# Retention and a routed mixture of experts on one core: slots by rank of the token count, experts chosen by register, short last blocks with slots as columns

## The chip, the cores and the metric

One NeuronCore of a Trainium2 chip runs the whole program. The metric is device time in microseconds of one execution, lower is better. The span is the stretch of a profiled execution in which the program's instructions run; the execution's own time is a little longer.

## The reference

Two stages. The first is attention without softmax, with a decay per head; the second sends each token to one expert. B, H, S, D = 4, 8, 576, 64; 2304 tokens of 512 features; 8 experts with inner size 1024; capacity 576.

```
scores = q k^T / sqrt(64);  ret = scores * gamma_h ** (i - j) for i >= j, else 0
x = (ret v), heads side by side                       # 2304 x 512
logits = x w_gate;  e(i) = argmax(logits_i);  p = softmax(logits)
slot of token i = number of earlier tokens with the same expert
h = relu(x w1[e]);  y = h w2[e];  out_i = p_i[e(i)] * y   # 0 where the slot is >= capacity
```

## The kernel before

**Attention stage (0 to 124 us).** A loop over 20 tiles of tokens (NTI; 5 of a batch, the last of them half full). Each tile's rows of x are written to DRAM (`xr`) as pairs of float16, high and low part, and turned for the gating logits. A batch's routing runs in steps (`route`, a generator) that the schedule calls at places named first, mid and late of later tiles: logits to one-hot rows, a count of earlier tokens by matmul, the slot of each token (`sr`), a block and row of it, and a matmul (psi) that adds token numbers to `maps`, from which `idx` (expert, block, row to token) is made. `weigh` does the same for the gate's weights with the tile `wals` and the matmul psw into `mapw`. All small matmul results of the routing (logits, psr, psi, psc, psw) are parts of one PSUM tile, `psl`. The instruction order of each engine is the order in which the code is written (a manual schedule).

**Expert stage.** Expert e has TE = 352 slots, in blocks of 128, 128 and 96 rows. `gather` fetches a block's rows from `xr` by `idx` with an indirect DMA on GpSimd (tile xg), `turn` turns them with a DMA transpose issued by SyncE (tile exT). `run` is one expert's work. First layer: for each of 8 groups f of hidden columns, 12 matmuls with a 128x128 weight tile as stationary operand and the slots as moving columns into one of three PSUM buffers `ph`; ScalarE makes hh, the high part, VectorE hl, the low part. Second layer: for each block r, 24 matmuls with the block's hh or hl as stationary operand and 512 weight columns moving into `py`; ScalarE scales it by the gate's weight (ot), GpSimd scatters it to `out`.

Between these steps `run` calls `piece(i)`: i = 0 to 7 after the groups of the first layer, 8 + 2r and 9 + 2r in the middle and at the end of block r. In the pieces the next expert is prepared. `split(e, i, j)` makes float16 high and low parts (wh on ScalarE, wl on VectorE) of half of weight part i (4 parts of 1 MB, w1 and w2 in halves); after a part's second half `fetch` starts the load of a further part into the pool `raw`, of 3 buffers, on SyncE's queue. `open_slots(e+1)`, at piece 8, gathers and turns the next expert's rows.

Expert 0 starts before the last batch is routed. Its first two blocks (256 slots, EARLY) hold tokens of the first three batches, and later tokens start at slot 256 (`shift`). The last batch's routing runs in its pieces (lists `between`), and then its third block and expert 1's rows are gathered (`tail_rows`). After the last expert nine small VectorE operations (`tot`, `exc`, `left`) find whether any token got no slot; every engine loads that number, and a further pass runs if it is above 0.

Of the kernel before, what the change touches and what calls it, by code (L numbers as in the profile page):

```python
# [18 lines left out]
P = 128  # L19
TE = 352  # L20
# [3 lines left out]
WEIGH = (("late", 5), ("mid", 6))  # L24
# [4 lines left out]
FETCH_LAST = 2  # L29
# [5 lines left out]
WEIGH_AT = (7, 8)  # L35
ROWS_AT = 7
WEIGHTS_AT = (8, 9, 9, 10, 24, 24, 24, 24)
EARLY = 256
# [7 lines left out]
def constants(B, H, S, D, E):  # L46
# [19 lines left out]
        "big": ones * np.full(nch, BIG)[None, :],  # L66
        "tok": np.stack([(tok - B * S) // 64 * 64, (tok - B * S) % 64], axis=2).reshape(P, -1),
# [11 lines left out]
def retention_moe(ctx, tc, q, k, v, w_gate, w1, w2, capacity, consts, where, out):  # L79
# [15 lines left out]
    raw_p = ctx.enter_context(tc.tile_pool(name="raw", bufs=3))  # L95
# [84 lines left out]
    swt = cpool.tile([P, E, NB], F32, tag="swt", name="swt")  # L180
    idx = cpool.tile([P, E, NB], I32, tag="idx", name="idx")

# [16 lines left out]
    raws, order_w = {}, [(e, i) for e in range(E) for i in range(4)]  # L199
# [213 lines left out]

    def route(b):
# [3 lines left out]
        if b == B - 1:  # L418
            nc.tensor.matmul(psc, ones, cnt, start=True, stop=True, skip_group_check=True)
            nc.vector.tensor_scalar(  # L420
                out=shift, in0=psc[:, 0:1], scalar1=-1.0, scalar2=float(EARLY), op0=ALU.mult, op1=ALU.add
            )
            nc.vector.tensor_scalar_max(shift, shift, 0.0)
# [31 lines left out]
        for c in range(NCH - 1):  # L455
            nc.tensor.matmul(
                psr[:, c + 1:, :], ones, oh[:, c:c + 1, :].to_broadcast([P, NCH - 1 - c, E]),
                start=False, stop=(c == NCH - 2), skip_group_check=True,
            )
        yield  # L460
# [19 lines left out]
        nc.vector.scalar_tensor_tensor(out=r0, in0=r0, scalar=-float(P), in1=sr, op0=ALU.mult, op1=ALU.add)  # L480
        cell = rt.tile([P, NCH, E, NB], F16, tag="cell", name="cell")
# [10 lines left out]
        yield  # L492
# [7 lines left out]
        for c in range(NCH):  # L500
            n = size[c]
            nc.tensor.matmul(
                psi, hot[:n, c, :], vals[:n, c].rearrange("p o w -> p (o w)"),
                start=(c == 0), stop=(c == NCH - 1), skip_group_check=True,
            )
        mv = maps.rearrange("p o e r -> p (o e r)")
        nc.vector.tensor_tensor(out=mv, in0=mv, in1=psi, op=ALU.add)
        if b >= B - 2:
            nc.vector.scalar_tensor_tensor(
                out=idx, in0=maps[:, 0], scalar=float(NT), in1=maps[:, 1], op0=ALU.add, op1=ALU.add  # L510
            )
        inc = rt.tile([P, E], F16, tag="inc", name="inc")
        with nc.allow_low_precision(reason="small integers"):
            nc.vector.tensor_reduce(out=inc, in_=oh.rearrange("p c e -> p e c"), axis=AX.X, op=ALU.add)
        nc.gpsimd.tensor_tensor(out=cnt, in0=cnt, in1=inc, op=ALU.add)
# [12 lines left out]
    def weigh(b):  # L528
# [15 lines left out]
        nc.vector.tensor_scalar_mul(parts[:, :, 2], isx.bitcast(I32), float(2.0 ** -23))  # L544
        wals = rt.tile([P, NCH, 3, E * NB], F16, tag="wals", name="wals")
# [15 lines left out]
        if b == B - 1:  # L561
            slot_weights(mapw, swt, [P, E, NB])

# [14 lines left out]

    blocks = [(r, r * P, min(P, TE - r * P)) for r in range(NB)]

# [7 lines left out]

    slots = {e: None for e in range(E)}
# [39 lines left out]
    for where_, d in WEIGH_NEXT:  # L629
        at(place[where_], t3 + d, lambda: next(weights[B - 2], None))  # L630
    order = ctx.enter_context(tc.manual_schedule())
    early = [x for x in blocks if x[1] < EARLY]
# [4 lines left out]

    at(mid, t3 + 3, early_rows)
# [46 lines left out]
    for _ in range(FETCH_LAST):  # L685
        fetch()
# [9 lines left out]
    def run(w, xT, c0, T, pieces, idc, wtc):  # L696
# [21 lines left out]
        for r in range(-(-T // P)):  # L718
            n = min(P, T - r * P)
# [8 lines left out]
            ot = ob_p.tile([P, DM], F32, tag="ot", name="ot")  # L728
            nc.scalar.activation(ot[:n], py[:n], AF.Copy, scale=wtc(r)[:n])  # L729
            nc.gpsimd.indirect_dma_start(  # L730
                out=out, out_offset=bass.IndirectOffsetOnAxis(ap=idc(r)[:n], axis=0),
                in_=ot[:n], in_offset=None, bounds_check=NT - 1, oob_is_err=False,
            )
            piece(KF + 2 * r + 1)

    def fast(e, r0, nb, pieces):
        T = min(TE, (r0 + nb) * P) - r0 * P
        run(
            ws[e], slots[e].xT, r0 * P, T, pieces,
            lambda r: idx[:, e, r0 + r:r0 + r + 1], lambda r: swt[:, e, r0 + r:r0 + r + 1],  # L740
# [8 lines left out]
    def open_slots(e):  # L749
        slots[e] = Slots(TE)  # L750
        gather(e, blocks)
        cross_rows(e, blocks)
# [4 lines left out]
    n_early = len(early)  # L757
    last = routes[B - 1]
    go = lambda: next(last, None)

    def fetch_last():
        for _ in range(3 - FETCH_LAST):
            fetch()
# [9 lines left out]
    between = [[] for _ in range(32)]  # L773
    for i, p in enumerate(CROSS_AT):
        between[p].append(lambda t=NTI - 2 + i: cross(t, ph_p))
    for i, p in enumerate(LOGITS_AT):
        between[p] += lg(3 - i)
    for i, p in enumerate(STAGES_AT):
        between[p].append(go)
    for p in WEIGH_AT:  # L780
        between[p].append(lambda: next(weights[B - 1], None))
    between[2].append(fetch_last)
    between[ROWS_AT].append(tail_rows)
    for i, p in enumerate(WEIGHTS_AT):
        between[p] += sp(1, i)
    fast(0, 0, n_early, [both(*between[i]) for i in range(12)])
    fast(0, n_early, NB - n_early, [both(*between[16 + i]) for i in range(10)])
    for e in range(1, E):
        pieces = []
        if e + 1 < E:  # L790
            pieces = [both(*sp(e + 1, p)) for p in range(8)]
            if e + 1 > 1:
                pieces.append(lambda e=e: open_slots(e + 1))
        fast(e, 0, NB, pieces)


    nc.tensor.matmul(psc, ones, cnt, start=True, stop=True, skip_group_check=True)
    tot = cpool.tile([P, E], F32, tag="tot", name="tot")
    exc = cpool.tile([P, E], F32, tag="exc", name="exc")
    nc.vector.tensor_scalar(out=tot, in0=psc, scalar1=cap[:, 0:1], scalar2=None, op0=ALU.min)  # L800
    nc.vector.tensor_tensor(out=exc, in0=psc, in1=tot, op=ALU.subtract)
    nc.vector.tensor_tensor(out=tot[:, 0:1], in0=tot[:, 0:1], in1=shift, op=ALU.add)
    nc.vector.tensor_scalar(out=tot, in0=tot, scalar1=-float(TE), scalar2=0.0, op0=ALU.add, op1=ALU.max)
    left = cpool.tile([P, E + 3], I32, tag="left", name="left")
    nc.vector.tensor_copy(left[:, 0:E], tot)
    nc.vector.tensor_reduce(out=left[:, E:E + 1], in_=tot, axis=AX.X, op=ALU.max)
    nc.vector.tensor_reduce(out=left[:, E + 2:E + 3], in_=exc, axis=AX.X, op=ALU.max)
    nc.vector.tensor_tensor(out=exc, in0=exc, in1=tot, op=ALU.max)
    nc.vector.tensor_reduce(out=left[:, E + 1:E + 2], in_=exc, axis=AX.X, op=ALU.max)
    any_left = nc.values_load(left[0:1, E + 1:E + 2], min_val=0, max_val=NT)  # L810
    with tc.If(any_left > 0):
# [18 lines left out]
        nc.vector.tensor_scalar_add(over, srs, -float(TE))  # L830
# [71 lines left out]
```

## Time and profile before

| | |
|---|---|
| time, median of 3 runs | 389.19 us (385.08 to 389.21) |
| the profiled execution | 385.27 us, span 383.5 us |
| TensorE busy | 353.4 us, 92% of the span |
| VectorE, ScalarE, GpSimd busy | 186.7, 177.4, 116.3 us |
| DMA | 69.62 MB, mean 182 GB/s |
| mean granted TensorE clock | 0.985 |

Matmuls overlap, so the durations of single ones add up to more than the busy time; what one costs in a stream is read from the distance between starts, or from the distance between the ScalarE operations that follow a group. A share over the whole span mixes the attention stage with the expert stage.

### The profile page before, as it was taken

The page shows a single profiled execution, that of the slowest core. Times are in us where ns is not written, and L with a number is a line of the kernel's source. Part 1 is how long each engine was busy: PE and PEld are TensorE (multiplying, and loading weights), DVE is VectorE, ACT ScalarE, POOL GpSimd, SP SyncE. Part 2 cuts the span into 40 slices and gives each one's busy share as a digit, 9 for nine tenths or more (in the row PEclk, how much of TensorE's full clock was granted, in tenths as well). Part 3 has the DMA queues.
Part 4 walks back from the last instruction along what each step waited for, and adds up shares of the span by engine and source line. Part 5 has one row for each costly group of instructions (what it writes and reads, how often), then busy time and mean ns, then how long its engine had stood idle before and what let it go on. Part 6 is the DMA issues. An engine that isn't in the chain of part 4 may idle for free.

```text
span 383.5 us, 8052 instructions
## 1 busy us (share of the span) xinstructions
PE 353.4 (92%) x3275; PEld 238.6 (62%) x3276; DVE 186.7 (49%) x376; ACT 177.4 (46%) x318; POOL 116.3 (30%) x132
## 2 busy tenths in 40 slices
PE   8899799899895979979989999999999989999990
PEld 4789689788785846645555466466456446556550
DVE  5444577778784565387058047228219308502101
ACT  2667567767463425394056156237137318412110
POOL 1384344654514046150151141133114116010020
PEclk9999989999998999999999999999999999999997
DMA  9999999898306638999939939839967984510010
GB/s 180 201 217 231 255 241 262 230 217 202 139 30 166 227 117 144 250 333 357 200 92 353 218 74 328 227 87 294 254 96 224 299 115 154 125 55 9 0 56 5
DMA packets 99753, 69.62 MB, mean 182 GB/s; under 512 B 82173, under 2 KB 82557, under 8 KB 99712
## 3 DMA queue, kind: packets, MB, share of 16 engines
q1 hardware_dynamic: 96096, 58.57, 60.9%
q0 software_dynamic: 3616, 10.49, 8.8%
q8 instruction: 27, 0.44, 0.5%
q14 instruction: 14, 0.11, 0.1%
HBM read 53.84 MB, written 10.49 MB: 168 GB/s over the span
## 4 chain that ended last, share of the span: by engine, by line
PE 59%; DMA 14%; DVE 9%; SPq 7%; ACT 5%; POOL 3%; issue 2%; POOLq 0%; ACTq 0%; DVEq 0%
DMA raw<-in_w 8%; PE ph L710 8%; PE ph L712 8%; PE ph L711 8%; PE py L723 7%; PE py L725 7%; PE py L724 7%; SPq L577 5%; DVE wl L228 4%; DMA exT<-xg 4%; PE px L344 4%; PE px L320 3%; PE pp L289 3%; ACT wh L227 3%; PE pt L381 2%
## 5 line engine op out<-in xcount | busy, mean ns | idle before, releaser
L228 DVE SCALAR_TENSOR_TENSOR wl<-raw,wh 128x1024 f16<-128x1024 f32 x64 | 79.5, 1247 | 30.0 <-ACT wh L227 26.5
L710 PE MATMUL ph<-exT,wh 128*128 128x352 f16 (+2 forms) x288 | 82.9, 296 | 4.8 <-DMA exT<-xg 2.6
L714 DVE SCALAR_TENSOR_TENSOR hl<-ph,hh 128x352 f16<-128x352 f32 (+2 forms) x72 | 34.5, 479 | 102.8 <-ACT hh L713 102.8
L712 PE MATMUL ph<-exT,wl 128*128 128x352 f16 (+2 forms) x288 | 82.9, 296 | 0.0
L711 PE MATMUL ph<-exT,wh 128*128 128x352 f16 (+2 forms) x288 | 82.9, 296 | 0.0
L730 POOL DMA_INDIRECT out<-ot,idx x24 | 25.6, 1068 | 170.3 <-ACT ot L729 111.1
L227 ACT ACTIVATE wh<-raw 128x1024 f16<-128x1024 f32 x64 | 66.9, 1052 | 16.6 <-DMA raw<-in_w 16.6
L723 PE MATMUL py<-wh,hh 128*128 128x512 f16 (+1 forms) x192 | 72.8, 379 | 0.0
L724 PE MATMUL py<-wl,hh 128*128 128x512 f16 (+1 forms) x192 | 72.8, 379 | 0.0
L725 PE MATMUL py<-wh,hl 128*128 128x512 f16 (+1 forms) x192 | 72.8, 379 | 0.0
L729 ACT ACTIVATE ot<-py,swt 128x512 f32<-128x512 f32 (+1 forms) x24 | 16.5, 686 | 91.7 <-PE py L725 69.1
L713 ACT ACTIVATE hh<-ph 128x352 f16<-128x352 f32 (+2 forms) x72 | 30.9, 430 | 40.5 <-PE ph L712 39.5
L710 PEld LDWEIGHTS <-wh 128*128 128x128 f16 x288 | 28.2, 98 | 16.0 <-DMA exT<-xg 4.0
L711 PEld LDWEIGHTS <-wh 128*128 128x128 f16 x288 | 28.1, 98 | 14.6 <-issue 2.8
L571 POOL DMA_INDIRECT xg<-xr,idx x24 | 33.9, 1412 | 7.8 <-issue 7.2
L712 PEld LDWEIGHTS <-wl 128*128 128x128 f16 x288 | 28.2, 98 | 11.9
L725 PEld LDWEIGHTS <-hl 128*128 128x128 f16 (+1 forms) x192 | 20.4, 106 | 21.1
L723 PEld LDWEIGHTS <-hh 128*128 128x128 f16 (+1 forms) x192 | 20.4, 106 | 20.5
L724 PEld LDWEIGHTS <-hh 128*128 128x128 f16 (+1 forms) x192 | 20.4, 106 | 20.2
L241 POOL TENSOR_TENSOR ks<-kn,cst 128x512 f32<-128x512 f32 (+1 forms) x19 | 21.2, 1117 | 33.6 <-DMA kn<-in_k 19.0
L294 DVE TENSOR_TENSOR pm<-pp,cst 128x512 f32<-128x512 f32 (+1 forms) x40 | 23.5, 627 | 1.3 <-PE pp L289 0.5
L344 PE MATMUL px<-vn,pm 128*64 128x64 f32 (+1 forms) x576 | 23.0, 224 | 0.0
(120 smaller groups left out, 393.2 us busy)
## 6 DMA issues: line engine op xcount, KB each, us to landing
raw<-in_w SPq DMA_DIRECT2D x32, 1024.0 KB, 7.1
qn<-in_q SPq DMA_DIRECT2D x16, 256.0 KB, 5.5
vn<-in_v SPq DMA_DIRECT2D x16, 256.0 KB, 5.3
xr<-xrow SPq DMA_DIRECT2D x16, 256.0 KB, 4.4
kn<-in_k SPq DMA_DIRECT2D x15, 256.0 KB, 5.0
kn<-in_k SPq DMA_DIRECT2D x6, 128.0 KB, 3.8
qn<-in_q SPq DMA_DIRECT2D x4, 128.0 KB, 4.3
vn<-in_v SPq DMA_DIRECT2D x4, 128.0 KB, 4.5
```

The source lines that it names most:

```text
L227: nc.scalar.activation(hv, raw[:, c], AF.Copy, scale=SW)
L228: nc.vector.scalar_tensor_tensor(out=lv, in0=raw[:, c], scalar=SW, in1=hv, op0=ALU.mult, op1=ALU.subtract)
L344: nc.tensor.matmul(px[z, h * D:(h + 1) * D], pm[h % 2][:n, h // 2, z], vn[:n, h, :], start=(c == 0 and h == 0), stop=(h == H - 1), skip_gr ...
L571: nc.gpsimd.indirect_dma_start(out=self.rows[:n, r, :].bitcast(I32), out_offset=None, in_=xr[:, :], in_offset=bass.IndirectOffsetOnAxis(ap ...
L710: nc.tensor.matmul(ph[:, :T], w.h1[:, kd, cols], xT[:, kd, z], start=(kd == 0), stop=False)
L711: nc.tensor.matmul(ph[:, :T], w.h1[:, kd, cols], xT[:, KD + kd, z], start=False, stop=False)
L712: nc.tensor.matmul(ph[:, :T], w.l1[:, kd, cols], xT[:, kd, z], start=False, stop=(kd == KD - 1))
L713: nc.scalar.activation(hh[:, f, :T], ph[:, :T], AF.Relu)
L714: nc.vector.scalar_tensor_tensor(out=hl[:, f, :T], in0=ph[:, :T], scalar=0.0, in1=hh[:, f, :T], op0=ALU.max, op1=ALU.subtract)
L723: nc.tensor.matmul(py[:n], hh[:, f, cols], w.h2[:, f, :], start=(f == 0), stop=False)
L724: nc.tensor.matmul(py[:n], hh[:, f, cols], w.l2[:, f, :], start=False, stop=False)
L725: nc.tensor.matmul(py[:n], hl[:, f, cols], w.h2[:, f, :], start=False, stop=(f == KF - 1))
```

## The change

- Slots by rank: `CAPS` = 372 for expert 0, then 368, 348, 324, 312, 296, 288, 280 for the other seven in the order of their token counts. The expert of rank 1 is chosen from the counts of three batches (`choose`, in piece 0 of expert 0), the others from all counts (`rank`, `rank_ids`, in piece 7). Small VectorE operations make the order, and `in_order` permutes `idx` and the weights by it. SyncE loads the experts' numbers into registers, and the weight loads take their addresses from them.
- Short last blocks: a last block of fewer than 112 slots (FEW) is computed with the roles exchanged: weight tiles of 128x128 stationary, the n slots moving (96 matmuls of n columns), then copied and turned back by four transposes in the middle of the following block (`rest`). This holds for ranks 2 to 7, with n = 92, 68, 56, 40, 32, 24. For expert 0 (116) and rank 1 (112) the last block is done as before.
- The pool `raw` has 4 buffers. The first three parts of rank 1 are fetched after `choose`. The gathers for the next expert stand at piece 0, the transposes at piece 3.
- The count of the last batch (`count_up`) stands earlier, the steps of `route` and `weigh` are cut at other places, and the test for tokens without a slot (`what_is_left`) stands in the first layer of expert 0's last block.

```diff
-TE = 352
+CAPS = (372, 368, 348, 324, 312, 296, 288, 280)
+TE = 384
-WEIGH_NEXT = (("late", 3), ("mid", 4))
+WEIGH_NEXT = ("late", 4)
+WEIGH_NEXT_AT = (0, 2)
-WEIGH_AT = (7, 8)
+WEIGH_AT = (7, 7, 8, 9)
+SPLITS_AT = (0, 1, 2, 3, 4, 5, 6, 7)
+OPEN_AT, TURN_AT = 0, 3
+FEW = 112
...
-    raw_p = ctx.enter_context(tc.tile_pool(name="raw", bufs=3))
+    raw_p = ctx.enter_context(tc.tile_pool(name="raw", bufs=4))
...
-            raws[order_w[0]] = load_raw(*order_w[0])
+            r, i = order_w[0]
+            raws[r, i] = load_raw(ereg[r], i)
...
+    def expert_at(r):
+        ereg[r] = nc.values_load(eids[0:1, r:r + 1], engines=(mybir.EngineType.SP,), min_val=0, max_val=E - 1)
+
+    def choose():
+        nc.tensor.matmul(psc, ones, cnt, start=True, stop=True, skip_group_check=True)
+        keys()
...
+        nc.vector.tensor_scalar(
+            out=shift, in0=psc[:, 0:1], scalar1=-1.0, scalar2=float(EARLY), op0=ALU.mult, op1=ALU.add
+        )
+        nc.vector.tensor_scalar_max(shift, shift, 0.0)
+        expert_at(1)
...
+        def rest(r, n):
+
+            cols = slice(r * P, r * P + n)
+            py = py_p.tile([P, KD, P], F32, tag="py", name="py")
+            for d in range(KD):
+                dm = slice(d * P, (d + 1) * P)
+                for f in range(KF):
+                    nc.tensor.matmul(py[:, d, :n], w.h2[:, f, dm], hh[:, f, cols], start=(f == 0), stop=False)
+                    nc.tensor.matmul(py[:, d, :n], w.l2[:, f, dm], hh[:, f, cols], start=False, stop=False)
+                    nc.tensor.matmul(py[:, d, :n], w.h2[:, f, dm], hl[:, f, cols], start=False, stop=(f == KF - 1))
...
+            nc.scalar.copy(yT[:, :, :n], py[:, :, :n])
+
+            def turn_back():
+                pt = py_p.tile([P, 512], F32, tag="py", name="pt")
+                for d in range(KD):
+                    nc.tensor.transpose(pt[:n, d * P:(d + 1) * P], yT[:, d, :n], ident)
+                out_rows(r, n, pt)
...
     def tail_rows():
-        gather(0, blocks[n_early:])
-        cross_rows(0, blocks[n_early:])
+        gather(0, blocks[0][n_early:])
+        cross_rows(0, blocks[0][n_early:])
+        rank()
         open_slots(1)
+        cross_rows(1, blocks[1])
+        rank_ids()
...
+    put(0, choose, fetch, fetch, fetch)
...
-    between[ROWS_AT].append(tail_rows)
+    put(ROWS_AT, tail_rows)
+    for p in WEIGH_AT:
+        put(p, lambda: next(weights[B - 1], None))
...
+    put(18, what_is_left)
```

The order of GpSimd's queue at the last batch's routing, before (cell and vals feed the psi matmuls, wals the psw matmuls, L571 gathers, L730 scatters):

```order
L483 TENSOR_TENSOR cell<-ohs,blk 128x120
L488 TENSOR_TENSOR vals<-cell,cst 128x5x24 x2
L515 TENSOR_TENSOR cnt<-cnt,inc 128x8
L547 TENSOR_TENSOR wals<-cell,pws 128x5x24 x3
L571 DMA xg<-xr,idx 96x512
L571 DMA xg<-xr,idx 128x512 x2
L571 DMA xg<-xr,idx 96x512
L730 DMA out<-ot,idx 2304x512 x3
```

The same place of GpSimd's queue after the change (L687 gathers, L838 scatters):

```order
L432 TENSOR_TENSOR cnt<-cnt,inc 128x8
L500 TENSOR_TENSOR cell<-ohs,blk 128x120
L505 TENSOR_TENSOR vals<-cell,cst 128x5x24 x2
L687 DMA xg<-xr,idx 128x512 x3
L687 DMA xg<-xr,idx 112x512
L566 TENSOR_TENSOR wals<-cell,pws 128x5x24 x3
L838 DMA out<-ot,idx 2304x512 x3
```

The three wals operations have moved behind the four gathers (one for expert 0's last block, three for rank 1).

VectorE's queue at the start of expert 0 after the change, from the last tile's xrow to the second group's hl (L828); key, top, picked, own, eids and shift are choose's:

```order
L380 SCALAR_TENSOR_TENSOR xrow<-px,sx,xrow 64x512
L828 SCALAR_TENSOR_TENSOR hl<-ph,hh 128x256
L592 SCALAR_TENSOR_TENSOR key<-psl,cst 128x8
L603 TENSOR_REDUCE top<-key 128x1
L604 TENSOR_TENSOR picked<-key,top 128x7
L606 TENSOR_TENSOR own<-picked,cst 128x7
L608 TENSOR_REDUCE eids<-own 128x1
L609 TENSOR_SCALAR shift<-psl 128x1
L612 TENSOR_SCALAR shift<-shift 128x1
L397 COPY xT<-pt 128x512
```

Before the change xrow, hl and xT stood there one behind the other, and two operations on shift four groups later; seven operations now stand between hl and xT, of which key and the first shift read `psl`.

TensorE's queue in the second layer of rank 2 after the change, where the full block ends and the short one begins (wh is the high part of the weights):

```order
L848 LDWEIGHTS hh
L848 MATMUL py<-wl_2879,hh 128x512
L849 LDWEIGHTS hl
L849 MATMUL py<-wh_2878,hl 128x512
L864 LDWEIGHTS wh_2878
L864 MATMUL py<-hh,wh_2878 128x92
L865 LDWEIGHTS wl_2879
L865 MATMUL py<-hh,wl_2879 128x92
L866 LDWEIGHTS wh_2878
L866 MATMUL py<-hl,wh_2878 128x92
```

The 92-column matmuls with weights as stationary operand, 96 of them, stand between the two full blocks; before, the queue went on with 512-column matmuls, and the third block with 24 of them stood last.

## Rows read from the trace of the kernel before

**Rows 1.** The page, parts 1 and 2: busy us, share of the span and instructions of each engine; the busy share of the DMA engines in tenths, in 40 slices of the span.

```profile
PE 353.4 (92%) x3275; PEld 238.6 (62%) x3276; DVE 186.7 (49%) x376; ACT 177.4 (46%) x318; POOL 116.3 (30%) x132
...
DMA  9999999898306638999939939839967984510010
```

**Rows 2.** Busy time by stretches of the span, one expert each: stretch, its length, busy us and count of PE, PEld, DVE, ACT and POOL, granted clock, DMA share, GB/s.

```profile
223.30:253.20 29.90, 29.90 (x170) 17.09 (x169) 13.28 (x16) 13.33 (x19) 7.46 (x7) 1.00 0.72 212
...
313.40:344.40 31.00, 30.05 (x170) 17.16 (x171) 13.37 (x16) 13.33 (x19) 9.36 (x7) 1.00 0.37 111
```

**Rows 3.** Timeline of ScalarE in the first layer, expert 0's last block (96 slots) and an expert of 352 slots: start us, us, engine, line, operation; in brackets the idle time before and what ended it.

```profile
152.41 0.25 ACT L713 ACTIVATE hh<-ph 128x96 f16<-128x96 f32 x1 [0.26 <-PE ph L712]
152.92 0.25 ACT L713 ACTIVATE hh<-ph 128x96 f16<-128x96 f32 x1 [0.26 <-PE ph L712]
...
287.10 0.47 ACT L713 ACTIVATE hh<-ph 128x352 f16<-128x352 f32 x1 [0.38 <-PE ph L712]
...
288.89 0.46 ACT L713 ACTIVATE hh<-ph 128x352 f16<-128x352 f32 x1 [0.38 <-PE ph L712]
```

**Rows 4.** Timeline of ScalarE at the end of the last expert's second and third block.

```profile
369.14 0.69 ACT L729 ACTIVATE ot<-py,swt 128x512 f32<-128x512 f32 x1 [4.49 <-PE py L725]
374.32 0.68 ACT L729 ACTIVATE ot<-py,swt 96x512 f32<-96x512 f32 x1 [4.49 <-PE psl L797]
```

**Rows 5.** Waits of TensorE: who waited for whom, us in total, times, longest; four rows of the whole span, and below the dots the first again from 100 us on.

```profile
PE psl L555 <- POOL wals L547: 6.4, 4, 4.1
PE ph L710 <- DMA exT<-xg: 2.6, 3, 1.3
PE ph L710 <- DVE hl L714: 2.2, 2, 1.4
PE psl L402 <- DVE mapw L560: 1.0, 1, 1.0
...
PE psl L555 <- POOL wals L547: 4.5, 2, 4.1
```

**Rows 6.** Short matmuls and their weight loads: two of the logits' matmuls on the timeline (six starts apart), two pieces of the chain of work that ended last (start us, us), and the group of weight loads of L710 (busy us, mean ns of one | idle before).

```profile
129.32 0.17 PE L406 MATMUL psl<-wgs,xT 128*128 128x8 f16 x1
...
129.47 0.17 PE L406 MATMUL psl<-wgs,xT 128*128 128x8 f16 x1
...
57.14 1.08 PE px L344 x32
58.83 0.59 PE pk L263 x4
...
L710 PEld LDWEIGHTS <-wh 128*128 128x128 f16 x288 | 28.2, 98 | 16.0 <-DMA exT<-xg 4.0
```

**Rows 7.** The transposes of the experts that start at 314.35 and 344.2 us: duration of the issue min/median/max in ns, first and last start, and us to landing; and the first gather for each on GpSimd's timeline.

```profile
288.03 1.06 POOL L571 DMA_INDIRECT xg<-xr,idx  x1 [0.30 <-issue]
...
L577 SPq DMA_TRANSPOSE exT<-xg x3: 1241/1295/6140, 301.8 to 309.4; - x3
...
DMA to landing us min/median/max: 4.9/9.2/10.7
...
320.13 1.61 POOL L571 DMA_INDIRECT xg<-xr,idx  x1 [0.31 <-issue]
...
L577 SPq DMA_TRANSPOSE exT<-xg x3: 1239/1264/1316, 329.1 to 331.8; - x3
...
DMA to landing us min/median/max: 2.9/3.3/3.4
```

**Rows 8.** The end of attention: busy time of one stretch (columns as in rows 2), TensorE's timeline around it, and the two transposes for expert 0's first blocks.

```profile
120.00:124.00 4.00, 4.00 (x40) 3.58 (x40) 0.50 (x2) 0.59 (x1) 0.00 (x0) 0.63 1.02 248
...
119.64 0.57 PE L555 MATMUL psl<-wals,hot 128*128 128x72 f16 x5 [4.09 <-POOL wals L547]
...
124.26 0.28 PE L710 MATMUL ph<-exT,wh 128*128 128x256 f16 x1
...
L577 SPq DMA_TRANSPOSE exT<-xg x2: 1232/1296/1360, 118.7 to 120.3; - x2
...
DMA to landing us min/median/max: 3.1/3.3/3.5
```

**Rows 9.** VectorE's timeline in the last routing: the first and the last of nine small dependent operations.

```profile
134.86 0.19 DVE L462 TENSOR_TENSOR sel<-psl,ohs 128x40 f32<-128x40 f32 x1
...
136.60 0.17 DVE L480 SCALAR_TENSOR_TENSOR r<-r,srs 128x5 f32<-128x5 f32 x1
```

**Rows 10.** The last routing: the psi matmuls, idx and wals on the timelines of their engines, and all gathers as a group (duration min/median/max in ns, first and last start).

```profile
138.49 0.38 PE L502 MATMUL psl<-vals,hot 128*128 128x48 f16 x5 [1.66 <-POOL vals L488]
...
139.15 0.18 DVE L509 SCALAR_TENSOR_TENSOR idx<-maps 128x24 int32<-128x24 f32 x1
...
140.79 1.08 POOL L547 TENSOR_TENSOR wals<-cell,pws 128x120 f16<-128x120 f16 x3 [0.99 <-DVE pws L540]
...
L571 POOL DMA_INDIRECT xg<-xr,idx x24: 998/1442/1926, 115.0 to 323.8; - x24
```

**Rows 11.** The end of the span: the last of the nine operations on VectorE, the last scatter on GpSimd, and SyncE's load of a number into a register (ns min/median/max).

```profile
375.71 0.16 DVE L809 TENSOR_REDUCE left<-exc 128x1 int32<-128x8 f32 x1
...
375.28 0.93 POOL L730 DMA_INDIRECT out<-ot,idx  x1 [4.20 <-ACT ot L729]
...
L810 SPq TENSOR_LOAD <-left x1: 467/467/467, 375.9 to 375.9; - x1
```

More of the change, by code (lines that the diff above doesn't have):

```diff
@@ L412, in retention_moe, with count_up @@
     sh = [P, NCH, E]
+    def count_up(oh):
+        inc = rt.tile([P, E], F16, tag="inc", name="inc")
+        with nc.allow_low_precision(reason="small integers"):
+            nc.vector.tensor_reduce(out=inc, in_=oh.rearrange("p c e -> p e c"), axis=AX.X, op=ALU.add)
+        nc.gpsimd.tensor_tensor(out=cnt, in0=cnt, in1=inc, op=ALU.add)
     def route(b):
@@ L508, in route @@
         if b >= B - 2:
+            a, z = (0, n_early) if b == B - 2 else (n_early, NB)
             nc.vector.scalar_tensor_tensor(
-                out=idx, in0=maps[:, 0], scalar=float(NT), in1=maps[:, 1], op0=ALU.add, op1=ALU.add
-            )
[L512 to L515, printed above, removed]
+                out=idx[:, 0, a:z], in0=maps[:, 0, 0, a:z], scalar=float(NT), in1=maps[:, 1, 0, a:z],
+                op0=ALU.add, op1=ALU.add,
+            )
+        if b < B - 1:
+            count_up(oh)
     routed = {}
@@ L587, in cross_rows @@
             slots[e].turn(r, n)
+    early = [x for x in blocks[0] if x[1] < EARLY]
+    n_early = len(early)
     slots = {e: None for e in range(E)}
@@ L636, in early_rows @@
         gather(0, early)
+    at(place[WEIGH_NEXT[0]], t3 + WEIGH_NEXT[1], lambda: next(weights[B - 2], None))
     at(mid, t3 + 3, early_rows)
@@ L717, in run, with out_rows, full @@
             piece(f)
-        for r in range(-(-T // P)):
-            n = min(P, T - r * P)
+            if f == 0 and turned_back:
+                turned_back.pop()()
+        def out_rows(r, n, py):
+            ot = ob_p.tile([P, DM], F32, tag="ot", name="ot")
+            nc.scalar.activation(ot[:n], py[:n], AF.Copy, scale=wtc(r)[:n])
+            nc.gpsimd.indirect_dma_start(
+                out=out, out_offset=bass.IndirectOffsetOnAxis(ap=idc(r)[:n], axis=0),
+                in_=ot[:n], in_offset=None, bounds_check=NT - 1, oob_is_err=False,
+            )
+        def full(r, n=P):
             py = py_p.tile([P, 512], F32, tag="py", name="py")
@@ L727, in run @@
                     piece(KF + 2 * r)
[L728 to L733, printed above, removed]
-            piece(KF + 2 * r + 1)
+                    if r and turned_back:
+                        turned_back.pop()()
@@ L736, in fast @@
+        whole, n = divmod(T, P)
+        few = 0 < n < FEW
+        for r in range(whole):
+            if few and r == min(1, whole - 1):
+                rest(whole, n)
+            full(r)
+        if few and not whole:
+            rest(0, n)
+        elif n and not few:
+            full(whole, n)
+    turned_back = []
     def fast(e, r0, nb, pieces):
-        T = min(TE, (r0 + nb) * P) - r0 * P
+        T = min(CAPS[e], (r0 + nb) * P) - r0 * P
+        wts = swt[:, 0] if e == 0 else sws[:, e - 1]
@@ L797, in retention_moe @@
[L797 to L809, printed above, removed]
+            for p, i in zip(SPLITS_AT, range(8)):
+                pieces[p] += sp(e + 1, i)
```

157 lines of the change are left out of this document (120 added, 37 removed).

## The prediction

> **What bounds the kernel now.** I read the page first: TensorE is busy for 353.4 us, 92% of the span [rows 1]. The busy time by stretches then says where this is a bound and not only a habit: an expert takes 29.9 us with TensorE busy for all of it, or 31.0 with 0.95 us of idle time, at clock 1.00, while VectorE, ScalarE and the DMA engines have slack [rows 2]. So in the expert stage time is columns. An expert's first layer gives a group of 12 matmuls every 1.79 us with 352 slots and every 0.51 us with 96 [rows 3]: 149 and 42.5 ns each, 0.417 ns per slot. Its second layer costs 5.18 us for a block of 24 matmuls of 512 columns, and the 96-slot block costs as much as a 128-slot one [rows 4]. Third I read TensorE's waits: 2.6 us for transposed rows (exT), 2.2 us for hl, 6.4 us for wals in the routing, 1.0 us for mapw [rows 5].
>
> **First layer: -9.1 us.** Slots go from 8 x 352 = 2816 to 2588, so 228 fewer. Each slot is a column of 96 matmuls: 228 x 96 x 0.417 ns = 9.1 us. This is on the path.
>
> **Second layer: -9.8 us.** Six experts (ranks 2 to 7) lose a 5.18 us block: -31.1. In its place come 96 matmuls of n = 92, 68, 56, 40, 32, 24 columns, every one with a fresh 128x128 weight tile. The nearest rows are the 96-column stream at 42.5 ns [rows 3] and the logits, eight pairs of load and matmul of 8 or 16 columns at 25 ns [rows 6]. So 92 columns cost 96 x 40.8 ns = 3.9 us and 68 cost 2.95 by the slope. For 56 and fewer something else paces: the logits say 25 ns, but there are only eight; 32 matmuls of 64 fp32 columns in a row took 1.08 us, 34 ns each [rows 6]. I take 28 ns, 2.7 us for each of four blocks. Together 17.7 us, with 16.5 (25 ns) and 24.5 (42.5 ns throughout) as ends. Turning a block back is four fp32 transposes; the four of L263 take 0.59 us [rows 6]: 6 x 0.6 = 3.6 us. The ScalarE copy of yT (about 0.6 us) lies beside half of the next full block (2.6 us), which covers it; uncovered it costs 3.6 us. Sum -31.1 + 17.7 + 3.6.
>
> The Trainium skill speaks against this part: "TensorE: Matmul & The Clock Gate", Back-to-back issue gap, gives about 81 ns for each matmul of 128 columns in a real stream of loads and matmuls. By that a short block would take 7.8 us and not 2.7 to 3.9, and the sum would end near 400 us. The trace differs: 42.5 ns at 96 columns over a whole layer; I follow the trace.
>
> **Feeding the experts: -4.8 us.** The hl waits (2.2 us) come in expert 1, where ScalarE stands behind a weight part that has not landed; the exT waits (2.6 us) come because the three transposes are issued behind four weight loads: those for the expert that starts at 314.35 were issued from 301.8 to 309.4, and the last landed 4.9 us later, at 314.3 [rows 7]. With a fourth raw buffer and the transposes moved to the third group, both sources go. What is late next is the chain gather, transpose, first matmul. In the expert that began at 314.35, with one weight load beside it, the chain took from 320.13 to 334.7 (331.8 + 2.9), 14.6 us [rows 7]; the last scatter of the expert before stands ahead of the gathers on GpSimd, hence the 5.8 us. An expert of 25.1 us, the shortest, leaves 19. I book both waits as gone, and a rival below is that they stay.
>
> **Attention: -2.0 us.** Two wals waits and the mapw wait behind them (6.4 - 4.5 = 1.9, and 1.0 [rows 5]) lose their cause, since the matmul on wals now stands behind the mix. The attention stage, the first third, also has its DMA engines full [rows 1], so I book 2.0 between 0 and 2.9.
>
> **Start of expert 0: +3.4 us.** The wals wait of 4.09 us at 119.64 goes. But the first expert matmul needs the transposes issued at 118.7 and 120.3, landing 3.5 and 3.1 us later, 123.4; it ran at 124.26 [rows 8]. So 0.8 us is won. TensorE will now be idle just before it: the 4.6 us of work from 119.64 on, most of it at a granted clock of 0.63, is 2.7 to 3 at full speed, and would be done by 118.5 (from 115.55). It was idle up to 119.64, and the next 4 us had a granted clock of 0.63 (a mean over the levels of 1.2 and 2.4 GHz), a loss of 1.5 us [rows 8]; such a loss now falls on expert 0. Net +0.7. Next, choose() puts a matmul and seven small VectorE operations behind the first group, and the logits behind it write the same PSUM tile as choose reads: they wait for the sixth. Small dependent operations take 0.21 us each (nine in 1.9 us [rows 9]), and hl stands ahead, so TensorE, done with its transposes in 0.6 us, waits about 1.7 us. In the third group the wals matmuls (0.3) and the mapw wait (0.5) now fall behind the start; the earlier count adds 0.2. Together 2.7. All of it delays the last routing.
>
> **Last routing: +6.3 us.** On GpSimd wals stood ahead of four gathers; now it stands behind them, and so do the five matmuls on wals, behind which TensorE's whole second layer is queued. Call the start of the psi matmuls P (138.49). idx was ready at P+0.8; rank adds eight small operations, 1.9 us, before the gathers of expert 1, which begin at P+2.9. A gather occupies GpSimd for 1.0 to 1.9 us, and 0.3 lie between two [rows 10]; VectorE stands still behind mapw in that time, so I take 1.0. Three end at P+6.8, wals takes 1.1 and ends at P+8.1. TensorE is there at P+0.3+2.6 and waits 5.2 us; now it waits 0.4 (4.5 - 4.1 [rows 5]). So +4.8, between 3 and 7. The wait is longer than the one at 119.64, so the clock falls again: +1.5, between 0 and 1.7.
>
> **The leftover count: +1.5 us.** Thirteen operations (some 2.5 us at the cadence of [rows 9]) move between hl of groups 3 and 4 of expert 0's last block, whose groups take 12 x 51 ns = 0.6 us. TensorE runs three PSUM buffers ahead, about 1 us beyond hl; so 1.5, between 0 and 2.5. At the end nothing is won: the last of the operations there ended at 375.87, before GpSimd had issued the last scatter (375.28 + 0.93) [rows 11].
>
> **At nothing:** the first three raw loads wait for a register (a load of one took 0.47 us [rows 11]) and choose, some 2 us; the six further register loads, 2.8 us and their checks, stand ahead of one raw load. Expert 0 now runs about 10 us longer, which covers both; without that cover some 3 us on ScalarE.
>
> Sum: -9.1 - 9.8 - 4.8 - 2.0 + 3.4 + 6.3 + 1.5 = -14.5. The profiled execution took 385.27 us for a span of 383.5: **370.8 us**. Two of the three timed runs took 389.2 and one 385.08, so a median may stand 4 us higher; that is inside the range.
>
> **Rivals.**
> (a) *The new waits at the start are hidden.* If POOL gets idx early and the count finds cover, 6.3, 1.5 and 1.7 go, and the time is near 361. For: GpSimd was idle most of that stretch. Against: in the order the four gathers plainly stand ahead of wals. 0.2.
> (b) *The experts wait for their rows.* Before, gather to last landing took 288.03 to 314.3, 26.3 us, with loads between [rows 7]. If that stays, a start comes some 30 us after the one before, as now: the forecast's experts of 29.0, 27.1, 26.4, 25.7 and 25.4 us lose 1.0, 2.9, 3.6, 4.3 and 4.6, and the time is 387, no change. Against: the 14.6 us chain. 0.1.
> (c) *Short matmuls are paced by their weight loads (slower).* A 128x128 load shows 98 ns [rows 6]. If loads were not hidden behind so few columns, a short block would take 96 x 98 ns = 9.4 us, and 56.4 for 17.7 gives 409 us. It decides from an average of 56 ns per short matmul, where the 14.5 us are used up (17.7 us are 31 ns each, and 14.5 us are 25). Against: logits at 25 ns with such loads. 0.06. The skill's 81 ns belongs to this case.
> (d) *The change doesn't do what it says*: a rank holds more tokens than its slots and the extra pass runs. One expert there loads, splits and multiplies with nothing beside it, so costs no less than the forecast's shortest expert, 25 us: beyond 395. The counts of the reference's inputs fit (335, 313, 292, 290, 287, 273, 255 against 368 to 280). 0.02.
>
> **How the numbers follow.** The forecast has 0.62: about 366 to 377 with the ends of short matmuls (-1.2, +6.8), attention and the waits. (a) reaches down to 360. Upward I go to 381, for the edge of the forecast with the 4 us by which timed runs differ; that leaves out (c), (d) and (b). A measurement of this kernel tells about 2% from no change, 377.6 us against the profiled execution. Faster: forecast, (a) and a part of (b), less the upper edge of the forecast: 0.83; within 2%: 0.10; slower: 0.07.
>
> **What would show it.** In the profile after: groups of 1.43 us in the last expert's first layer; short blocks of 2.7 to 3.9 us; no exT wait from rank 2 on; one TensorE wait of about 5 us for wals with the clock low behind it; one of under 2 us at the first logits of expert 0. Wrong would be: experts of equal length near 29 us (b), short blocks over 5.2 us (c).

## The result and the profile after

The changed kernel takes 372.19 us (median of four runs, 371.23 to 372.38); runs of the kernel before beside it took 389.2 (385.08 to 392.96). The ratio is 0.959, 95% interval 0.952 to 0.967. Run again beside other kernels, below called the control, it took 373.88 us, ratio 0.966 (0.960 to 0.971).

The profiled execution of after took 372.29 us, its span is 370.4. Its page, where [rows 1] stood before: busy us, share and instructions of TensorE, its weight loads and VectorE, and the granted clock in 40 slices.

```profile
PE 334.7 (90%) x3731; PEld 241.1 (65%) x3732; DVE 188.0 (51%) x397; ACT 177.7 (48%) x324; POOL 113.5 (31%) x132
...
PEclk9999999999999589699999999999999999999996
```

TensorE is busy for 18.7 us less (353.4 before), but the end moved by only 13.1 us: 5.6 us are new idle time. Beside it the granted clock dips twice, around 125 and 152 us, and work at a lower clock counts as busy all the same. Five stretches of TensorE in each kernel (length, busy us and count, granted clock, DMA share, GB/s): up to the first matmul of expert 0, its first two blocks, its third, ranks 1 to 7, the end. Before:

```profile
0.00:124.26 124.26, 110.28 (x1777) 0.97 0.85 198
124.26:150.18 25.92, 23.90 (x204) 1.00 0.53 168
150.18:159.44 9.26, 9.26 (x122) 1.00 1.04 151
159.44:374.07 214.63, 209.82 (x1177) 1.00 0.65 183
374.07:383.50 9.43, 0.17 (x2) 0.76 0.02 5
```

After:

```profile
0.00:122.70 122.70, 106.48 (x1773) 1.00 0.87 199
122.70:161.24 38.54, 30.51 (x207) 0.79 0.53 162
161.24:172.55 11.31, 10.23 (x122) 1.00 0.72 262
172.55:359.61 187.06, 187.06 (x1633) 1.00 0.64 188
359.61:370.40 10.79, 0.38 (x2) 0.70 0.07 26
```

Ranks 1 to 7 take 27.6 us less and hold no wait at all. Expert 0 takes 49.85 us for 35.18, so 14.7 us are given back there. TensorE's waits of after from 118 us on (who waited for whom, us in total, times, longest), to be read against [rows 5]:

```profile
PE ph L824 <- DMA exT<-xg: 5.1, 1, 5.1
PE psl L574 <- POOL wals L566: 4.7, 1, 4.7
PE psl L518 <- POOL vals L505: 1.7, 1, 1.7
PE ph L824 <- DVE hl L828: 1.1, 1, 1.1
PE psl L416 <- DVE shift L609: 1.1, 1, 1.1
PE psl L416 <- DVE mapw L579: 0.6, 1, 0.6
```

The first stands before expert 0 (in place of the 4.09 us of [rows 8]); the others lie in it, in the order vals, wals, then hl behind the leftover count; shift and mapw are at the logits of the first and third group. What two of these waits do to the clock:

```profile
122.70:131.87 9.17, 8.11 (x50) 0.50 0.40 128
131.87:142.94 11.07, 8.80 (x101) 1.00 0.55 216
150.75:155.77 5.02, 5.02 (x16) 0.50 1.05 228
```

Behind the wait for exT TensorE works 8.1 us at the half level, behind that for wals 5.0 us; I put the loss at half of each, 6.6 us together: the 256-column matmuls start every 0.21 us before 131.87 and every 0.11 us behind it.

The second layer of rank 7 on ScalarE's timeline of after, as [rows 4] before: start us, us, operation, and in brackets the idle time and what ended it.

```profile
352.06 0.69 ACT L837 ACTIVATE ot<-py,sws 128x512 f32<-128x512 f32 x1 [4.83 <-PE py L849]
354.39 0.24 ACT L870 COPY yT<-py 128x96 f32<-128x96 f32 x1 [1.65 <-PE py L866]
357.48 0.68 ACT L837 ACTIVATE ot<-pt,sws 24x512 f32<-24x512 f32 x1 [2.85 <-PE pt L875]
360.07 0.69 ACT L837 ACTIVATE ot<-py,sws 128x512 f32<-128x512 f32 x1 [1.91 <-PEq L962]
```

Read on ScalarE, the short block takes 2.33 us (352.06 to 354.39), and the full block with the turning back in its middle 5.68 for 5.18: turning back costs 0.5 us. The copy is long done by then. By the starts of TensorE's matmuls the six short blocks take 3.96, 2.99, 2.48, 2.41, 2.40 and 2.40 us, 16.6 together; this reading is used below.

### The profile page after: what moved, and what is told of

It reads as the page before. It is cut to its first block, busy times and chain, and to the rows that moved or that the text cites. A ratio compares the mean times of both kernels' runs of the same rounds, so it can differ in the third digit from the quotient of the medians.

```text
span 370.4 us, 9065 instructions
## 1 busy us (share of the span) xinstructions
PE 334.7 (90%) x3731; PEld 241.1 (65%) x3732; DVE 188.0 (51%) x397; ACT 177.7 (48%) x324; POOL 113.5 (31%) x132
## 3 DMA queue, kind: packets, MB, share of 16 engines
q0 software_dynamic: 3904, 10.14, 8.3%
## 5 line engine op out<-in xcount | busy, mean ns | idle before, releaser
L824 PE MATMUL ph<-exT,wh 128*128 128x256 f16 (+8 forms) x288 | 82.0, 291 | 6.1 <-DMA exT<-xg 5.1
L828 DVE SCALAR_TENSOR_TENSOR hl<-ph,hh 128x256 f16<-128x256 f32 (+8 forms) x72 | 32.4, 453 | 102.8 <-ACT hh L827 102.8
L825 PE MATMUL ph<-exT,wh 128*128 128x256 f16 (+8 forms) x288 | 82.0, 291 | 0.0
L826 PE MATMUL ph<-exT,wl 128*128 128x256 f16 (+8 forms) x288 | 81.9, 291 | 0.0
L838 POOL DMA_INDIRECT out<-ot,idx x24 | 26.3, 1094 | 156.2 <-ACT ot L837 119.7
L847 PE MATMUL py<-wh,hh 128*128 128x512 f16 (+2 forms) x144 | 55.6, 386 | 0.0
L848 PE MATMUL py<-wl,hh 128*128 128x512 f16 (+2 forms) x144 | 55.5, 385 | 0.0
L849 PE MATMUL py<-wh,hl 128*128 128x512 f16 (+2 forms) x144 | 55.3, 384 | 0.0
L827 ACT ACTIVATE hh<-ph 128x256 f16<-128x256 f32 (+8 forms) x72 | 29.6, 410 | 44.2 <-PE ph L826 36.8
L687 POOL DMA_INDIRECT xg<-xr,idx x24 | 29.8, 1241 | 9.3 <-issue 7.0
L849 PEld LDWEIGHTS <-hl 128*128 128x128 f16 (+2 forms) x144 | 14.8, 103 | 17.1 <-issue 1.1
L847 PEld LDWEIGHTS <-hh 128*128 128x128 f16 (+2 forms) x144 | 14.8, 102 | 14.9 <-issue 1.0
L848 PEld LDWEIGHTS <-hh 128*128 128x128 f16 (+2 forms) x144 | 14.8, 103 | 14.7 <-issue 0.8
L255 POOL TENSOR_TENSOR qs<-qn,cst 128x512 f32<-128x512 f32 (+1 forms) x18 | 23.7, 1314 | 1.6 <-DMA qn<-in_q 1.1
```

What stands on the lines that cost most here:

```text
L255: eng.tensor_tensor(out=to[:n, h0:h1], in0=x[:n, h0:h1], in1=tab[:n, c, h0:h1].unsqueeze(2).to_broadcast([n, h1 - h0, D]), op=ALU.mult,)
L687: nc.gpsimd.indirect_dma_start(out=self.rows[:n, r, :].bitcast(I32), out_offset=None, in_=xr[:, :], in_offset=bass.IndirectOffsetOnAxis(ap ...
L824: nc.tensor.matmul(ph[:, :T], w.h1[:, kd, cols], xT[:, kd, z], start=(kd == 0), stop=False)
L825: nc.tensor.matmul(ph[:, :T], w.h1[:, kd, cols], xT[:, KD + kd, z], start=False, stop=False)
L826: nc.tensor.matmul(ph[:, :T], w.l1[:, kd, cols], xT[:, kd, z], start=False, stop=(kd == KD - 1))
L827: nc.scalar.activation(hh[:, f, :T], ph[:, :T], AF.Relu)
```

## The experiments

Ten traces with the same code up to there (after, the control and eight variants) reached expert 0 at 122.6 to 126.9 us. That spread of 4.3 us is larger than most effects below, so each is read from the first matmul of expert 0 on, and the times stand beside it.

**The control, and a pause in the short blocks.** No edit.

> The changed kernel unaltered, as a control for the others of this group. In three of the four kernels so far each short block of 24 to 56 columns held one pause of 0.4 to 0.5 us, about 70 matmuls in, that waited for nothing the profile shows; the first profile of the changed kernel had none. If the pause belongs to those kernels' code, it is absent here and the six short blocks take 16.3 to 16.7 us, 372.2. If it belongs to the chip or the run, it may be here too: short blocks of 18.4 us and about 374.

373.88 us. Ranks 1 to 7 took 188.64 us, 1.6 more than in the first profile, and the six short blocks 18.2 us for 16.6. TensorE's timeline in the block of 56 columns:

```profile
278.51 0.19 PE L865 MATMUL py<-hh,wl 128*128 128x56 f16 x1
278.91 0.20 PE L866 MATMUL py<-hl,wh 128*128 128x56 f16 x1 [0.21 <-issue]
```

Starts come every 25 to 26 ns, then, behind the 83rd of the 96, one 0.40 us later, with no semaphore behind it. Counted so, the pause in blocks of 24 to 56 columns lies behind 80 to 86 matmuls in every profile that has it, not behind some 70 as the expectations say. So the pause belongs to the run and not to the variants' code; the first profile happened to have none.

**wals ahead of the gathers.**

```diff
+    for p in WEIGH_AT[:2]:
+        put(p, lambda: next(weights[B - 1], None))
     put(ROWS_AT, tail_rows)
-    for p in WEIGH_AT:
+    for p in WEIGH_AT[2:]:
         put(p, lambda: next(weights[B - 1], None))
```

> In the last routing the two VectorE and GpSimd stages of the weights (wals) are put ahead of the four gathers; nothing else moves. Theory, the place in GpSimd's queue makes the wait: TensorE's wait of 4.70 us for wals falls below 1 us (0.36 before the change), the half clock of 6.8 us behind it goes (2.5 us), and the time falls from 372.2 to about 365. Rival, the inputs of wals (its exponentials and sums on ScalarE and VectorE) are late and not its turn: a wait of 3 us or more stays, and the time is 371 or more. A second rival: the gathers, now behind wals, come 1 to 2 us later, and expert 0's last block (161.24) or rank 1 (172.55) waits for exT by as much.

369.87 us, ratio 0.953 (0.944 to 0.961). GpSimd's timeline in the last routing, after and then this variant:

```profile
144.14 1.03 POOL L687 DMA_INDIRECT xg<-xr,idx  x1 [1.26 <-DVE key L627]
...
148.58 1.01 POOL L687 DMA_INDIRECT xg<-xr,idx  x1 [0.30 <-issue]
149.62 1.07 POOL L566 TENSOR_TENSOR wals<-cell,pws 128x120 f16<-128x120 f16 x3
```

```profile
147.03 1.09 POOL L566 TENSOR_TENSOR wals<-cell,pws 128x120 f16<-128x120 f16 x3 [2.32 <-DVE pws L558]
148.31 1.04 POOL L687 DMA_INDIRECT xg<-xr,idx  x1 [0.19 <-issue]
```

TensorE's wait for wals in the variant, and its stretch behind that wait:

```profile
PE psl L574 <- POOL wals L566: 0.3, 1, 0.3
```

```profile
148.17:153.00 4.83, 4.83 (x26) 1.00 0.37 109
```

The wait is 0.3 us and the clock behind it 1.00. Expert 0 took 41.0 us: 4.4 and 2.5 of the 8.9 us come from this, the rest from a clock that was back 3.3 us after the start. The rivals are out: the wait for wals went with its turn, and no exT wait appeared behind the start of expert 0. The total fell short of 365 because this run reached expert 0 3.9 us later and had the pauses.

**TensorE kept busy before expert 0.**

```diff
+    busy = psA.tile([P, NP, P], F32, tag="pp0", name="busy")
+    for _ in range(22):
+        nc.tensor.matmul(
+            busy.rearrange("p a b -> p (a b)"), idle[:, 0:P], idle, start=True, stop=True, skip_group_check=True
+        )
     actx.close()
```

> Twenty-two matmuls of 512 columns on a tile of zeros, which nothing reads, are added on TensorE between the end of attention and expert 0, where it stood idle for 5.06 us (22 x 0.213 = 4.7 us). Theory, the clock: the half level from 121.6 to 131.9 follows from that idle time, and TensorE works there from 122.7 on; with the idle time filled the granted clock stays at 1.00, expert 0's first groups come at twice the pace, and 9.17 / 2 less the wait of 1.06 inside it, some 4 us, are won: 368. Rival, the chain of the last routing (choose, logits, VectorE, GpSimd) sets the pace and not TensorE: the clock stays high, but the waits at the logits and for vals (1.06, 0.56, 1.71) grow by what is won, and the time stays at 371.5 or more.

373.26 us. Stretches from the start of expert 0, of this variant and of the control:

```profile
125.55:131.87 6.32, 4.85 (x53) 1.00 0.30 71
...
142.43:150.23 7.80, 4.79 (x19) 0.76 0.44 114
```

```profile
123.74:127.53 3.79, 3.62 (x21) 0.50 0.32 99
127.53:141.89 14.36, 11.20 (x127) 1.00 0.58 220
```

The clock at the start follows from the idle time, as the theory has it: with it filled the half level is gone. The wait for vals did not grow (1.7), that for shift did, by 0.4, and the wait for wals was 3.0 us for 4.7. Expert 0 took 45.98 us, 3.9 less than in after, but the control, where the half level lasted 3.8 us and not 9.2, took 48.29, so 2.3 less than that; the clock fell later instead, behind the wait for vals. In the time it does not show, since this run reached expert 0 1.8 us later than the control; its attention stage had ended 1.9 us later, ahead of the added matmuls.

**The leftover count later.**

```diff
-    put(18, what_is_left)
+    put(24, what_is_left)
```

> The thirteen operations of the leftover count are moved from between hl of the third and fourth group of expert 0's last block to the middle of that block's second layer. Theory: the wait of 1.08 us at 166.15 goes and nothing takes its place, 371.1. Rival: VectorE is as full there (four weight splits of 1.27 us each), and hl of rank 1's first groups comes late by as much: a wait of about 1 us in rank 1 and 372.2.

374.71 us, no gain to be measured. But expert 0's last block took 10.18 us with no wait (11.31 in after, 11.77 in the control), and rank 1 30.50 as there. The theory holds in its place, 1.1 to 1.6 us.

**Second layer and first layer, each undone.**

```diff
-FEW = 112
+FEW = 0
```

> The six short last blocks run as before the change, with the slots as rows and 24 matmuls of 512 columns; everything else as changed. Theory, the whole of the second layer's gain is on the path: six blocks of 5.18 us (31.1) come back for 16.3 us of short matmuls and 2.9 us of turning back, so 11.9 us more, less up to 0.8 us at the end, where the last scatter is a small one again: 383 to 384. Rival, longer experts hide waits that now cost something (feeding the experts), so less than 9 us: below 381.

384.63 us, and for the second, which adds `CAPS = (372, 368, 368, 368, 368, 368, 368, 368)`:

> No slots by rank: every rank has 368, and no short blocks; the last blocks of 112 slots run with slots as rows. The step on the first layer says that a slot costs 96 matmul columns of 0.417 ns: 360 slots more than in the kernel without short blocks (384.6) cost 14.4 us, each rank takes 30.5 us, and the time is 399. If a first layer of few columns were paced by something else, the ranks with 280 and 288 slots gained less by their fewer slots and the difference is under 13 us: below 397.5.

400.25 us, ratio to before 1.037 (1.029 to 1.046). Ranks 1 to 7 without short blocks, and two of the ranks with 368 slots:

```profile
173.03:372.66 199.63, 199.63 (x1177) 1.00 0.63 177
```

```profile
176.28:206.78 30.50, 30.50 (x170) 1.00 0.92 268
359.28:389.56 30.28, 30.28 (x168) 1.00 0.06 20
```

Short blocks are worth 12.6 us against the first profile of after and 11.0 against the control with its pauses; fewer slots by rank 13.7 (six at 30.50 and the last 30.28 are 213.3, less 199.6), where 14.4 were expected. Together that is 26.2 us of the 26.3 expected (14.4 and 11.9); why the kernel between lies 0.7 us off is open. Both gains are on the path in full.

**Feeding the experts.** Three variants: three raw buffers for four (`bufs=3`); gathers and transposes late (`OPEN_AT, TURN_AT = 8, 8`); both.

> Three raw weight buffers as before the change, not four; the transposes stay in the third group. Theory A, the fourth buffer took away the waits in expert 1: hl waits of about 2.2 us are back there (rank 1 takes 32.7 us or more for 30.5), 374.5. Theory B, the place of transposes and gathers did it all: rank 1 takes 30.5, no wait comes back, the same time as the control.

> Gathers and transposes for the next expert are put in the middle of the first full block of the second layer, where the gathers stood before the change; four raw buffers stay. From there an expert has 10.3 to 11.7 us left; three gathers (1.0 to 1.3 each), the landing, three transpose issues (1.25 each) and their 3 us to landing make about 9.7, and weight loads stand ahead on SyncE. Theory, the place of the transposes matters: TensorE waits for exT by 1 to 3 us at the start of ranks 4 to 7, 4 to 10 us together. Rival, there is enough slack even there: no exT wait over 0.5 us and the time of the control.

> Three raw weight buffers and gathers and transposes in the middle of the first full block, both as before the change. Either of the two alone brought no wait back. Theory, each of the two is enough by itself to keep the transposes from standing behind a blocked weight load: with both undone exT waits of 0.3 to 1.3 us are back at the starts of ranks 2 to 7, 2.6 us or more together, as before the change, since the experts are shorter now. Rival, the waits came from something else (expert 0 was shorter, and the first weights of the next experts landed late): no exT wait over 0.3 us, and ranks 1 to 7 take within 0.5 us of the control's 188.6.

375.44, 376.17 and 380.88 us. Neither alone brought a wait back: rank 1 took 30.50 us in both, and no start waited for exT. With both undone the waits came back (waits of TensorE from 173 us on, and the stretches of ranks 5 and 6):

```profile
PE ph L824 <- DMA exT<-xg: 3.6, 2, 2.1
```

```profile
288.96:316.89 27.93, 25.61 (x245) 1.00 0.76 214
316.89:343.92 27.03, 26.80 (x245) 0.94 0.35 106
```

The longer wait, before rank 6, cost 1.7 us more by the clock (second stretch, 27.03 for 25.33 in the control). Ranks 1 to 7 took 194.45 us for the control's 188.64. So either edit is enough, and together they prevent 5.8 us. The hl waits in rank 1 of before did not come back even with both; they went with something else. The three raw loads at the start of expert 0 are one candidate; that was not tried.

**What a short matmul costs.**

```diff
-                    nc.tensor.matmul(py[:, d, :n], w.h2[:, f, dm], hh[:, f, cols], start=(f == 0), stop=False)
...
+                for h in (slice(0, 64), slice(64, P)):
+                    dm = slice(d * P + h.start, d * P + h.stop)
+                    for f in range(KF):
+                        nc.tensor.matmul(py[h, d, :n], w.h2[:, f, dm], hh[:, f, cols], start=(f == 0), stop=False)
...
```

> In the short blocks of the changed kernel each matmul with a 128x128 weight tile becomes two with 128x64 halves of it, into the two halves of the PSUM tile: 192 matmuls for 96, the same products. What sets the 24 to 25 ns of a matmul of 24 to 56 columns? Theory A, a price for each pair of load and matmul, whatever its size: 192 x 24.5 = 4.7 us for each of the four shortest blocks and 7.7 and 5.9 us for those of 92 and 68 columns, with longer pauses besides: 16 us or more over the control's 373.9. Theory B, the weight columns that are loaded: half of them take half the time, the four shortest blocks stay at 2.4 to 2.8 us, and only the two long ones, which their columns pace, get longer, by up to 3.9 and 2.9 us: 374 to 381.

399.52 us. The blocks of 40 and 24 slots, 192 matmuls each:

```profile
317.43:322.92 5.49, 5.49 (x194) 1.00 0.74 233
373.40:378.88 5.48, 5.48 (x193) 1.00 0.14 51
```

28.5 ns per matmul: half the weight columns do not halve the price. That is theory A, which had put it at 24.5, and theory B is out. It does not say whether the load or the issue sets it: by the Trainium skill, "TensorE: Matmul & The Clock Gate", Weight-path perf modes, the fast weight load needs all 128 columns, so a load of 64 may be a slower kind; no row here separates the two. On the timeline of weight loads one of 64 columns shows 0.11 us (262.72) and one of 128 columns 0.10 (254.10). In the block of 68 columns TensorE stood still once for 2.9 us on "issue", up to 262.71, while the DMA engines were full and one packet of the instruction queue moved; that the short pauses too are late instructions is possible and not shown.

**All edits together, and fewer short matmuls.** The first has the three edits above, and choose() copies the counts out of PSUM once (`held`). The second also merges, up to 64 slots, two of the three matmuls:

```diff
+                        nc.tensor.matmul(
+                            py[:, d, :2 * n].rearrange("p (o n) -> p o n", o=2), w.h2[:, f, dm], hx[:, f, :, cols],
+                            start=(f == 0), stop=False,
+                        )
+                        nc.tensor.matmul(
+                            py[:, d, :n], w.l2[:, f, dm], hh[:, f, cols], start=False, stop=(f == KF - 1)
+                        )
...
+                nc.vector.tensor_tensor(out=yT[:, :, :n], in0=yT[:, :, :n], in1=py[:, :, n:2 * n], op=ALU.add)
```

> All edits together: wals ahead of the gathers, the 22 matmuls that keep TensorE busy before expert 0, the leftover count in the middle of the second layer of expert 0's last block, and choose() copies the counts out of PSUM once, so that the logits behind it wait for one VectorE operation and not for the sixth. Theory, the four costs are separate: expert 0 takes 49.85 us in the changed kernel and then 4.4 + 2.5 (wals wait and its clock) + 4.1 (clock at the start) + 1.1 (count) + 0.8 (choose) less, some 37 us, and the time is 360 to 361. Rival, the chain of the last routing takes what TensorE gains: the wait for vals grows from 1.71 us to 3 or 4, expert 0 takes 39 to 40 us, and the time is 363 to 364.

> As the kernel with all edits, and in the short blocks of up to 64 slots hh and hl stand side by side as one moving operand for the high part of the weights: 64 matmuls for 96 (32 of 2n columns and 32 of n), with one VectorE addition of the two halves before the block is turned back. Theory, a short matmul costs what its weight load and issue cost, about 25 ns up to 56 columns, and the pause of 0.4 us comes only after some 70 of them in a row: blocks of 24, 32 and 40 slots take 1.6 to 2.0 us for 2.8, the one of 56 about 2.5 for 2.9, no pause in them, 3 us less together: 362.9. Rival, columns set the price, or the addition on VectorE (behind weight splits of 1.27 us) comes too late for the turn back in the middle of the next block: under 1 us is won, 365 or more.

365.88 us (0.943, 0.939 to 0.947) and 362.33 us (0.940, 0.935 to 0.944): both faster than the two kernels of the case. With all edits expert 0 takes 39.65 us, where the rival had put it, but not for the rival's reason: the wait for vals stayed at 1.7, and the clock fell behind it (0.94 over the first two blocks):

```profile
124.50:154.03 29.53, 26.07 (x207) 0.94 0.61 169
154.03:164.15 10.12, 10.12 (x121) 1.00 0.60 166
```

The time of 365.88 is above both forecasts: against the first profile of after this run reached expert 0 1.8 us later, and its ranks 1 to 7, with the pauses, took 1.8 us more.

The blocks of 24, 32, 40 and 56 slots, merged, and in the second box those of 56 and 24 with all edits but the merging:

```profile
340.26:341.86 1.60, 1.60 (x65) 1.00 0.00 0
316.28:318.03 1.75, 1.75 (x66) 1.00 0.02 5
291.77:293.72 1.95, 1.95 (x65) 1.00 0.72 151
266.50:268.90 2.40, 2.40 (x66) 1.00 0.80 226
```

```profile
268.77:271.66 2.89, 2.65 (x97) 1.00 0.74 235
...
344.88:347.64 2.76, 2.55 (x97) 1.00 0.02 6
```

64 matmuls of 48 and 24 columns take 25 ns each: up to some 56 columns the number counts, not the columns. The pause is gone from these four blocks, which have no more than 64 matmuls. Ranks 1 to 7 took 186.07 us for 188.89, so 2.8 of the 3 us expected were won.

## Why the prediction was right, and where it was not

Predicted 370.8, measured 372.19 and 373.88, in the range and near its middle. That the sum came so near is in part luck, since its misses have both signs: ranks 1 to 7 gained 3.1 us more than forecast (1.5 in the control), and expert 0, the way up to it and the end took that back and 1.4 us (2.5) more. By stretches, as changes in us of the profiled spans:

| | predicted | after | control |
|---|---|---|---|
| up to expert 0 (attention -2.0, start -0.8) | -2.8 | -1.6 | -0.5 |
| expert 0 | +12.8 | +14.7 | +13.1 |
| ranks 1 to 7 | -24.5 | -27.6 | -26.0 |
| end | 0 | +1.4 | +1.4 |
| sum | -14.5 | -13.1 | -12.0 |

**First layer.** Right. The last group of rank 7 (280 slots) on ScalarE's timeline of after:

```profile
346.83 0.40 ACT L827 ACTIVATE hh<-ph 128x280 f16<-128x280 f32 x1 [1.03 <-PE ph L826]
```

0.40 and 1.03 us of idle time before it are the 1.43 us per group that were forecast. The slots by rank alone are 13.7 for 14.4.

**Second layer.** Right in mechanism, the forecast's price near: 16.6 us in the first profile and 18.2 with the pauses, for 17.7. The floor was 24 to 25 ns and not 28 (the logits' 25 ns of [rows 6] were the better row), the pause was not foreseen, and turning back cost 0.5 and not 0.6 us. Rival (c) is out. The 81 ns for 128 columns of the Trainium skill ("TensorE: Matmul & The Clock Gate", Back-to-back issue gap) do not hold for these streams: 40 ns at 92 columns, 51 ns at 116 (first layer of expert 0's last block). The table of that section, about 25 ns as an issue floor up to 64 columns, agrees with the 24 to 26 ns from 24 to 56 columns.

**Feeding.** The waits went, and the ranks fall from 30.5 to 24.4 us as they should, which rules out (b) and (d); (a) falls with the waits of 4.7 and 1.1 us in expert 0. But the step credited the two edits jointly with both; either is enough for exT, and the hl waits had another cause, which stays open.

**Attention.** The step cannot be told: two wals waits and the mapw wait went, but waits for kT (1.2 us) and lg (1.35) came, and the same code varies by 4.3 us.

**Expert 0.** The waits were sized well: shift 1.06 for 1.7, mapw 0.56 for 0.5, wals 4.7 for 5.2, the count 1.08 for 1.5; they came out somewhat smaller, which hides a part of what follows. The term that failed is the clock. The step booked 1.5 us behind each idle stretch, from the one row of [rows 8], with an upper end of 1.7 for the second; after lost 4.1 and 2.5, because the half level lasted 9.2 us of expert 0 and not about 3. Run to run that length differs (3.8 in the control; more on it at the end), so a single row was no bound.

**End.** Booked as zero, it costs 1.4 us. The last block is a full one now; its scatter on GpSimd's timeline of after, against [rows 11]:

```profile
361.26 1.00 POOL L838 DMA_INDIRECT out<-ot,idx  x1 [1.88 <-ACTq L962]
```

It starts 1.19 us after ot and not 0.96, and moves 128 rows and not 96; from start to landing it took 2.9 us, the one before 2.0. Without short blocks, with 24 rows last, the end took 10.14 us and not 10.79, so about half may be the size; the rest is open. One candidate, not tested: on the chain that ended last GpSimd's load of `left` into a register (0.49 us, from 361.05) now stands ahead of that scatter, there too without short blocks; before the change it did not.

## What to carry over

When work moves on a queue, price the wait of whoever stands behind it, and then the slow clock after the wait: here it cost another 6.6 us. An in-order queue that feeds the critical engine's next step (wals) should hold nothing longer ahead of it (the gathers), even if that is needed soon. Where matmuls are short, count them before you count columns: 64 of 48 and 24 columns beat 96 of 24.

## What was not expected of the hardware

After the same idle time of 5.1 to 5.3 us the half clock lasted 3.0 to 4.0 us into expert 0 in four of the ten traces and 7.9 to 9.3 in the other six:

```profile
126.61:129.90 3.29, 3.29 (x20) 0.50 0.38 117
```

That is the variant with wals first; after shows 9.17. The rows show one thing that goes with it, when in the idle time the clock fell. The last 5 us before expert 0, in after and in the control:

```profile
117.70:122.70 5.00, 0.00 (x1) 0.89 0.85 201
```

```profile
118.60:123.74 5.14, 0.02 (x2) 0.70 0.80 201
```

A mean of 0.89 means the half level for the last 1.1 us, one of 0.70 for the last 3.1 us. Read the same way, the fall came 2.8 to 3.8 us before expert 0 in the four traces in which the half level then lasted 3.0 to 4.0 us, and 0.9 to 2.3 us before it in the six in which it lasted 7.9 to 9.3. A late fall thus went with a long slow start; why is not shown.

And a run of matmuls 24 to 26 ns apart is broken behind 80 to 86 of them by one pause of 0.35 to 0.5 us, in every profile with 96 in a row but the first. At 30 ns (68 columns) three of ten profiles have one of 0.3 us, at 40 ns (92 columns) none.
